# FFN first half: splitting the next block's input weights ahead of the block, and adding the second half of the converted weights behind that split

## The chip, the cores and the metric

The kernel runs on one core of one Trainium2 chip. The metric is the device time of one execution in microseconds. Before the change three executions took 719.34, 719.35 and 721.04 us (median 719.35 us).

## What is computed

A clustered attention feeds a two-layer FFN with a learned slope for negative values, and that feeds a routed mixture of experts. The change lies in the FFN:

```python
def _moe_ref(x, w_in, w_out, alpha):          # x 1536 x 512, w_in 512 x 2048, w_out 2048 x 512
    h = x @ w_in
    g = np.maximum(h, 0.0) + alpha * np.minimum(h, 0.0)
    return (g @ w_out).astype(np.float32)
```

The weights arrive as 64-bit words (float64 values). [...]

## The kernel before

**Tiles.** The 2048 hidden columns are 16 blocks `f` of 128. The 1536 tokens are two halves `gi` of 768, and a half is two chunks `c` of 384. The first half (`gi` 0) goes over all 16 blocks, then the second half does. The change is in the loop over the blocks 2 to 15 of the first half.

**One block on TensorE (PE).** `hidden(0, f, ...)` makes `h` for chunk 0 and chunk 1: each is 12 matmuls (line 677), four with the high input weights `wh` and the high tokens, four with `wh` and the low tokens, four with the low weights `wl`. The two PSUM tiles `h` come from a pool of two buffers, so chunk c of block f+1 needs the tile that chunk c of block f left. Then `second(0, f - 1)` adds 18 matmuls (line 726) of the block before to six sums `y`.

**One chunk on the other engines.** VectorE (DVE) makes `gm` from `h` (lines 702 and 703; the last reader of `h` is line 703), ScalarE (ACT) rounds it to `gh` (line 705), DVE subtracts: `gl = gm - gh` (line 707).

**Conversion.** `convert(f + 2)` stands behind chunk 1 of block f. It works in two halves of 128x512: q = 0 are the block's input weights, q = 1 its output weights. ACT takes the absolute value (line 569) and the top bits (line 570), DVE clamps (571), shifts (573) and joins (575), and GpSimd (POOL) adds the two pieces (line 577). `word` is a generator with these steps, and `convert` steps both halves in turn:

```python
            for _ in range(4):
                for g in gs:
                    next(g, None)
```

**Split.** `split(f, o, eng)` makes `wh` on ACT (line 648) and `wl = w - wh` on `eng` (line 649); o = 0 are the input weights, o = 1 the output weights. In the loop `eng` is GpSimd. Behind chunk 0 of block f stand `split(f + 1, 0)` and `split(f, 1)`.

**What sets the order.** Each engine works through its own queue in the order in which the code issues instructions; `hidden` calls `after(c)` behind each chunk. SP's queue brings a block's 64-bit weights with `load(f + 5)`, behind `hidden`.

Of the kernel before, what the change touches and what calls it, by code (L numbers as in the profile page):

```python
# [543 lines left out]
class Convert:  # L544
# [10 lines left out]
    def load(self, f):  # L555
        raw = self.slot(f)
        self.nc.sync.dma_start(out=raw[:, :DM].rearrange("p (k n) w -> p k (n w)", k=DM // P), in_=self.w_in[:, :, f])
        self.nc.sync.dma_start(out=raw[:, DM:].rearrange("p n w -> p (n w)"), in_=self.w_out[:, f])
# [53 lines left out]
def ffn(tc, A, cst, xs, xp, y1d, R, cv, W32, fw, ps_h, spare, more):  # L612
# [5 lines left out]
    nc = tc.nc  # L618
    ident, wg, LG = cst["ident"], cst["wg"], R["LG"]
    KD = DM // P  # L620
    NF = DFF // P
# [8 lines left out]
    def convert(f):  # L630

        if f < NF:
            gs = [cv.word(f, slice(q * DM, (q + 1) * DM), ck.tile([P, DM], I32, tag="ct", name="ct")) for q in range(2)]
            for _ in range(4):
                for g in gs:
                    next(g, None)

    ws, gs, over = {}, {}, {}

    def split(f, o, eng, gi=0):  # L640

        if o == 1 and gi == 1 and NF - TAIL <= f < NF - 2:
            wh, wl = over["xl"].pop(0), over["xl"].pop(0)
        else:
            wh = fw.tile([P, DM], F32R, tag=f"wh{o}", name=f"wh{o}")
            wl = fw.tile([P, DM], F32R, tag=f"wl{o}", name=f"wl{o}")
        w = W32(f)[:, o * DM:(o + 1) * DM]
        nc.scalar.copy(wh, w)
        eng.tensor_tensor(out=wl, in0=w, in1=wh.bitcast(F32), op=ALU.subtract)  # L649
        ws[f, o] = (wh, wl)  # L650
# [7 lines left out]
    def hidden(gi, f, eng, after, between=lambda: None):  # L658
        for _ in hiddens(gi, f, eng, after, between):
            pass  # L660

    def hiddens(gi, f, eng, after=lambda c: None, between=lambda: None, act=False):
# [17 lines left out]
        for c in range(2):  # L680
# [29 lines left out]
            if not act or f + c == 2:  # L710
                pay()
            after(c)
            if c == 1:
                gs[f] = (gh, gl)
# [4 lines left out]
    def second(gi, f, ns=range(3), ts=range(GT)):  # L719
        wh, wl = ws[f, 1]  # L720
        gh, gl = gs[f]
        for n, (a, w) in enumerate(((gh, wh), (gh, wl), (gl, wh))):
            for t in ts if n in ns else ():
                if f == 0 and n == 0:
                    ys[gi * GT + t] = ps_y.tile([P, DM], F32, tag="y", name="y")
                nc.tensor.matmul(ys[gi * GT + t], lhsT=a[:, t * P:(t + 1) * P], rhs=w,  # L726
                                 start=(f == 0 and n == 0), stop=(gi == 0 and f == NF - 1 and n == 2))
        if ns[-1] == 2 and ts[-1] == GT - 1:
            del ws[f, 1], gs[f]
# [60 lines left out]
    for f in (4, 5, 6):  # L790
        load(f)
    convert(3)
    second(0, 0)
    for f in range(2, NF):

        def after(c):
            if c == 0:
                split((f + 1) % NF, 0, nc.gpsimd)
                split(f, 1, nc.gpsimd)
            else:  # L800
                convert(f + 2)

        hidden(0, f, nc.vector, after)
        if f + 5 < NF:
            load(f + 5)
        second(0, f - 1)
# [742 lines left out]
def kernel(ctx, tc, A):  # L1549
# [164 lines left out]
    def begin():  # L1714
        ps_h = c2.enter_context(tc.tile_pool(name="ps_h", bufs=2, space=PSUM, side="right", reuse_waits="tile"))
        fw = c0.enter_context(tc.tile_pool(name="ffw", bufs=2, side="right", reuse_waits="tile"))
        return ffn(tc, A, cst, xs, xp, y1d, R, cv, lambda f: w32[f], fw, ps_h, spare, lambda *a: got.append(a) if a else more())
# [108 lines left out]
```

## Time and profile before

| | |
|---|---|
| median of three executions | 719.35 us |
| profiled execution, its own time | 718.92 us |
| its span in the trace | 717.1 us |
| attention with the FFN's first two blocks beside its end | to 263.5 us |
| blocks 2 to 15 of the first half of the tokens | 263.5 to 382.0 us |
| second half of the tokens | 382 to 504 us |
| routing and experts | from 504 us |

The profiled execution's time is 1.8 us more than its span (what lies around the span), and 0.43 us under the median. The page's first part gives each engine's busy time. A timeline row gives start, duration, engine, line, operation, and in brackets how long the engine was idle before it and who ended that.

### The profile page before, as it was taken

How to read it: one execution, taken by the hardware profiler on the slowest of the kernel's cores; microseconds unless marked ns; L12 is line 12 of the kernel's file. 1: busy time of each engine (PE TensorE's matmuls, PEld its weight loads, DVE VectorE, ACT ScalarE, POOL GpSimd, SP SyncE). 2: the span in 40 equal slices, each digit the busy share in tenths (PEclk: the TensorE clock that was granted, in tenths of full speed). 3: DMA queues.
4: the chain of work that ended last, by engine and by line, in shares of the span. 5: the costliest groups of instructions: out<-in, count | busy, mean ns of one | idle time of the engine just before them, and what ended most of it. 6: DMA issues, size and time to landing. Idle time of an engine off the chain costs nothing.

```text
span 717.1 us, 11778 instructions
## 1 busy us (share of the span) xinstructions
PE 699.9 (98%) x4111; PEld 625.8 (87%) x4111; DVE 568.2 (79%) x1114; ACT 472.1 (66%) x905; POOL 381.9 (53%) x339
## 2 busy tenths in 40 slices
PE   8999999999999999999999999999999999999995
PEld 5998989989999899888889999999888989898884
DVE  6989988898989878788784989976468888785651
ACT  6889788888889954554545655556645867574640
POOL 4659779697896386666662000001025888884201
PEclk9999999999999999999999999999999999999998
DMA  7867666676765133333203600026444999996000
GB/s 204 213 160 177 133 166 157 156 173 127 169 164 123 41 115 122 133 138 136 119 1 122 188 0 1 1 64 202 147 149 139 385 367 320 353 352 262 33 10 25
DMA packets 43904, 108.42 MB, mean 151 GB/s; under 512 B 8698, under 2 KB 24522, under 8 KB 38464
## 3 DMA queue, kind: packets, MB, share of 16 engines
q1 hardware_dynamic: 36768, 67.03, 34.4%
q0 software_dynamic: 7072, 40.60, 15.3%
q8 instruction: 34, 0.56, 0.3%
q14 instruction: 30, 0.25, 0.1%
HBM read 74.78 MB, written 10.10 MB: 118 GB/s over the span
## 4 chain that ended last, share of the span: by engine, by line
PE 66%; DVE 8%; DMA 8%; ACT 6%; POOL 6%; issue 5%; POOLq 0%; SPq 0%; ACTq 0%; DVEq 0%
PE h L677 18%; PE y L726 16%; DMA raw<-in_wall_dram,wi 7%; PE yo L1210 5%; PE pt L342 4%; PE hw L1263 4%; PE h L1210 3%; PE s L308 2%; PE px L360 2%; DVE nm L324 2%; PE y L736 2%; ACT e L331 2%; PE s L311 2%; DVE etl L345 2%; PE px L362 2%
## 5 line engine op out<-in xcount | busy, mean ns | idle before, releaser
L345 DVE TENSOR_TENSOR etl<-pt,eth 128x384 fp32r<-128x384 f32 x192 | 101.9, 549 | 19.6 <-ACT eth L344 18.4
L344 ACT CAST eth<-pt 128x384 fp32r<-128x384 f32 x192 | 90.9, 485 | 19.4 <-PE pt L342 19.4
L1177 POOL DMA_INDIRECT xg<-y1d,gi x16 | 27.8, 1738 | 130.5 <-DVE gi L1026 113.8
L342 PE MATMUL pt<-ident,e 128*128 128x128 f32 x576 | 93.8, 272 | 0.3 <-ACT e L331 0.3
L331 ACT ACTIVATE e<-s,nm 128x768 f32<-128x768 f32 x96 | 87.4, 910 | 6.4 <-DVE nm L324 5.6
L324 DVE TENSOR_REDUCE nm<-s 128x1 f32<-128x768 f32 x96 | 90.5, 943 | 0.9 <-PE s L311 0.8
L705 ACT CAST gh<-gm 128x384 fp32r<-128x384 f32 x60 | 30.8, 513 | 81.8 <-DVE gm L703 58.5
L342 PEld LDWEIGHTS pt<-ident,e 128*128 128x128 f32 x576 | 73.6, 140 | 7.0 <-ACT e L331 0.6
L707 DVE TENSOR_TENSOR gl<-gm,gh 128x384 fp32r<-128x384 f32 x60 | 49.4, 824 | 25.7 <-ACT gh L705 25.7
L360 PE MATMUL px<-etl,vh 128*64 128x384 f32 (+1 forms) x192 | 65.5, 368 | 1.5 <-DVE etl L345 1.3
L308 PE MATMUL s<-AB 128*128 128x384 f32 x192 | 57.5, 381 | 2.5 <-ACT e L331 2.1
L577 POOL TENSOR_TENSOR pre<-ct,pre 128x512 int32<-128x512 int32 x26 | 37.2, 1451 | 35.8 <-DVE ct L575 35.8
L677 PE MATMUL h<-xh,wh 128*128 128x384 f32 x256 | 55.6, 338 | 0.6 <-DVE gm L700 0.4
L677 PE MATMUL h<-xh,wl 128*128 128x384 f32 x256 | 56.0, 339 | 0.0
L677 PE MATMUL h<-xl,wh 128*128 128x384 f32 x256 | 55.0, 336 | 0.0
L362 PE MATMUL px<-eth,vh 128*128 128x384 f32 x160 | 54.0, 337 | 0.0
L1545 DVE TENSOR_TENSOR wl<-raw,wh 128x2048 fp32r<-128x2048 f32 (+2 forms) x26 | 44.5, 1717 | 11.7 <-ACT wh L1541 11.7
L311 PE MATMUL s<-CD 128*128 128x384 f32 x192 | 49.3, 338 | 1.0 <-DVE CD L439 1.0
L677 PEld LDWEIGHTS h<-xh,wh 128*128 128x128 f32 x256 | 45.5, 188 | 3.3 <-DVE gm L700 0.5
L677 PEld LDWEIGHTS h<-xh,wl 128*128 128x128 f32 x256 | 44.6, 188 | 2.7 <-POOL wl L649 2.6
L677 PEld LDWEIGHTS h<-xl,wh 128*128 128x128 f32 x256 | 45.7, 188 | 0.0
L1541 ACT CAST wh<-raw 128x2048 fp32r<-128x2048 f32 (+2 forms) x26 | 37.4, 1444 | 10.6 <-PE yo L1210 10.6
(357 smaller groups left out, 1816.8 us busy)
## 6 DMA issues: line engine op xcount, KB each, us to landing
AB<-RL SPq DMA_DIRECT2D x31, 384.0 KB, 5.3
raw<-in_w_in_dram SPq DMA_DIRECT2D x16, 512.0 KB, 4.0
raw<-in_w_out_dram SPq DMA_DIRECT2D x16, 512.0 KB, 4.7
raw<-in_wall_dram SPq DMA_DIRECT2D x8, 1024.0 KB, 8.2
Tp<-in_qkT_dram SPq DMA_DIRECT2D x16, 384.0 KB, 4.1
CD<-RL SPq DMA_DIRECT2D x15, 384.0 KB, 6.9
raw<-in_wall_dram POOLq DMA_DIRECT2D x4, 1024.0 KB, 11.8
vt<-in_v_dram SPq DMA_DIRECT2D x8, 384.0 KB, 6.3
```

The costliest lines, as they stand in the source:

```text
L308: nc.tensor.matmul(s[:, u, :384], lhsT=AB[:, 0, t * P:(t + 1) * P], rhs=AB[:, 1, ks], start=True, stop=False)
L311: nc.tensor.matmul(s[:, u, :384], lhsT=CD[:, 0, t * P:(t + 1) * P], rhs=CD[:, 1, ks], start=False, stop=True)
L324: nc.vector.tensor_reduce(out=nm, in_=s[:, :, :384], axis=AX.XY, op=ALU.max, negate=True)
L331: nc.scalar.activation(e.rearrange("p (u c) -> p u c", u=2), s[:, :, :384], AF.Exp, bias=nm, accum_out=den[:, i % 3:i % 3 + 1])
L342: nc.tensor.transpose(pt[:, i2], e[:, kt * P:(kt + 1) * P], ident)
L344: nc.scalar.copy(eh, pt)
L345: lows[u] = lambda: nc.vector.tensor_tensor(out=etl[:, 3 * u:3 * u + 3, q * P:(q + 1) * P], in0=pt, in1=eh.bitcast(F32), op=ALU.subtract)
L360: nc.tensor.matmul(px[:m], lhsT=vh[:, kt, :m], rhs=etl[:, kt], start=False, stop=False)
L362: nc.tensor.matmul(px, lhsT=vh[:, kt, :], rhs=eth[:, kt], start=False, stop=(kt == NT - 1))
L677: nc.tensor.matmul(hs[c], lhsT=a[:, k * P:(k + 1) * P], rhs=x[:, k, c * HC:(c + 1) * HC], start=(k == 0 and i == 0), stop=(k == KD - 1 and ...
L726: nc.tensor.matmul(ys[gi * GT + t], lhsT=a[:, t * P:(t + 1) * P], rhs=w, start=(f == 0 and n == 0), stop=(gi == 0 and f == NF - 1 and n == 2))
L1210: nc.tensor.matmul(out, lhsT=l[:, k], rhs=r[:, k * DM:(k + 1) * DM], start=start and k == 0 and i == 0, stop=stop and k == 3 and i == len( ...
```

## The change

`convert` leaves out the last step (the POOL add) of its second half and keeps its generator in `sums`. At the head of the loop's body, before `hidden`, now stand `split(f + 1, 0)` (until now behind chunk 0) and, behind it, that add. `split(f, 1)` stays behind chunk 0. No instruction is added or removed, and none changes its operands or size.

```diff
         if f < NF:
             gs = [cv.word(f, slice(q * DM, (q + 1) * DM), ck.tile([P, DM], I32, tag="ct", name="ct")) for q in range(2)]
-            for _ in range(4):
-                for g in gs:
+            for n in range(4):
+                for g in gs if n < 3 else gs[:1]:
                     next(g, None)
-
+            sums.append(gs[1])
+
+    sums = []
...
         def after(c):
             if c == 0:
-                split((f + 1) % NF, 0, nc.gpsimd)
                 split(f, 1, nc.gpsimd)
             else:
                 convert(f + 2)
 
+        split((f + 1) % NF, 0, nc.gpsimd)
+        for g in sums:
+            next(g, None)
+        sums.clear()
         hidden(0, f, nc.vector, after)
```

In the changed file lines 648, 649, 705 and 707 are 650, 651, 707 and 709.

On ACT, from the conversion of block 5 to the second chunk of block 4, before (`ct`, `pre`: the conversion; `gh`: chunk 0, then chunk 1 of block 4; the first `wh` is block 5's input weights, the second block 4's output weights; what stands in brackets is whose signals an instruction waits for):

```order
L569 ACTIVATE ct<-raw_3816 128x512 [waits DMAHW2_49,Pool_49]
L570 ACTIVATE pre_3818<-raw_3816 128x512
L705 CAST gh<-gm 128x384 [waits DVE_49,PE_49,Activation_49]
L648 CAST wh_4059<-pre_3818 128x512 [waits Pool_49]
L648 CAST wh_4063<-pre_3818 128x512 [waits PE_49]
L705 CAST gh<-gm 128x384 [waits DVE_49]
```

The same place on ACT in the changed kernel:

```order
L569 ACTIVATE ct<-raw_3816 128x512 [waits DMAHW2_49,Pool_49]
L570 ACTIVATE pre_3818<-raw_3816 128x512
L650 CAST wh_4038<-pre_3818 128x512 [waits PE_49,Pool_49]
L707 CAST gh<-gm 128x384 [waits DVE_49,PE_49,Activation_49]
L650 CAST wh_4063<-pre_3818 128x512 [waits PE_49]
L707 CAST gh<-gm 128x384 [waits DVE_49]
```

The `wh` of the next block's input weights, which waits for POOL, has moved from behind `gh` of chunk 0 to ahead of it.

On POOL, the conversions of blocks 5 and 6 and the splits around them, before:

```order
L577 TENSOR_TENSOR pre_3818<-ct,pre_3818 128x512 [waits DVE_49,Activation_49] x2
L649 TENSOR_TENSOR wl_4060<-pre_3818,wh_4059 128x512 [waits PE_49,Activation_49]
L649 TENSOR_TENSOR wl_4064<-pre_3818,wh_4063 128x512 [waits Activation_49]
L577 TENSOR_TENSOR pre_3819<-ct,pre_3819 128x512 [waits DVE_49,Activation_49] x2
L649 TENSOR_TENSOR wl_4140<-pre_3819,wh_4139 128x512 [waits PE_49,Activation_49]
L649 TENSOR_TENSOR wl_4144<-pre_3818,wh_4143 128x512 [waits Activation_49]
```

The same place on POOL in the changed kernel:

```order
L577 TENSOR_TENSOR pre_3818<-ct,pre_3818 128x512 [waits DVE_49,Activation_49]
L651 TENSOR_TENSOR wl_4039<-pre_3818,wh_4038 128x512 [waits PE_49,Activation_49]
L577 TENSOR_TENSOR pre_3818<-ct,pre_3818 128x512 [waits DVE_49]
L651 TENSOR_TENSOR wl_4064<-pre_3818,wh_4063 128x512 [waits Activation_49]
L577 TENSOR_TENSOR pre_3819<-ct,pre_3819 128x512 [waits DVE_49,Activation_49]
L651 TENSOR_TENSOR wl_4119<-pre_3819,wh_4118 128x512 [waits PE_49,Activation_49]
L577 TENSOR_TENSOR pre_3819<-ct,pre_3819 128x512 [waits DVE_49]
L651 TENSOR_TENSOR wl_4144<-pre_3818,wh_4143 128x512 [waits Activation_49]
```

The second add of each conversion has moved behind the low part of the input weights; PE's and DVE's own orders are as before.

## Rows read from the trace of the kernel before

**Rows 1.** The page, part 1: busy time, share of the span, instructions.

```profile
PE 699.9 (98%) x4111; PEld 625.8 (87%) x4111; DVE 568.2 (79%) x1114; ACT 472.1 (66%) x905; POOL 381.9 (53%) x339
```

**Rows 2.** Busy time by stretch: PE, PEld, DVE, ACT, POOL, granted clock, DMA share.

```profile
263.50:382.00 118.50, 118.50 (x589) 105.36 (x588) 97.07 (x163) 59.12 (x110) 79.86 (x58) 1.00 0.28 98
```

**Rows 3.** PE timeline, blocks 2 to 15: start, duration, line, operation.

```profile
263.50 0.87 PE L677 MATMUL h<-xh,wh 128*128 128x384 f32 x4
...
271.81 0.87 PE L677 MATMUL h<-xh,wh 128*128 128x384 f32 x4
...
347.92 0.86 PE L677 MATMUL h<-xh,wh 128*128 128x384 f32 x4
348.62 0.86 PE L677 MATMUL h<-xl,wh 128*128 128x384 f32 x4
349.41 0.97 PE L677 MATMUL h<-xh,wl 128*128 128x384 f32 x4
...
373.52 0.87 PE L677 MATMUL h<-xh,wh 128*128 128x384 f32 x4
...
375.82 0.85 PE L677 MATMUL h<-xh,wh 128*128 128x384 f32 x4
```

**Rows 4.** Who waited for whom, 246 to 382 us: total, times, longest.

```profile
PEld h L677 <- POOL wl L649: 2.6, 10, 0.3
```

**Rows 5.** POOL timeline: the first and the last conversion's adds (blocks 3 and 15).

```profile
268.23 2.86 POOL L577 TENSOR_TENSOR pre<-ct,pre 128x512 int32<-128x512 int32 x2 [1.70 <-DVE ct L575]
...
370.52 2.87 POOL L577 TENSOR_TENSOR pre<-ct,pre 128x512 int32<-128x512 int32 x2 [2.82 <-DVE ct L575]
```

**Rows 6.** POOL timeline from block 12's conversion on; the x2 row begins with the x1 row.

```profile
344.94 1.61 POOL L577 TENSOR_TENSOR pre<-ct,pre 128x512 int32<-128x512 int32 x1 [2.84 <-DVE ct L575]
346.51 1.28 POOL L577 TENSOR_TENSOR pre<-ct,pre 128x512 int32<-128x512 int32 x1
347.76 1.60 POOL L649 TENSOR_TENSOR wl<-pre,wh 128x512 fp32r<-128x512 f32 x1
347.76 2.85 POOL L649 TENSOR_TENSOR wl<-pre,wh 128x512 fp32r<-128x512 f32 x2
```

**Rows 7.** DVE timeline over the same block: end of block 12's conversion, block 11's chunks.

```profile
344.11 1.29 DVE L575 SCALAR_TENSOR_TENSOR ct<-raw,ct 128x512 int32<-128x512 int32 x2
344.71 0.69 DVE L575 SCALAR_TENSOR_TENSOR ct<-raw,ct 128x512 int32<-128x512 int32 x1
...
345.96 0.56 DVE L703 SCALAR_TENSOR_TENSOR gm<-h,gm 128x384 f32<-128x384 f32 x1
347.17 1.04 DVE L707 TENSOR_TENSOR gl<-gm,gh 128x384 fp32r<-128x384 f32 x1 [0.66 <-ACT gh L705]
...
348.77 0.56 DVE L703 SCALAR_TENSOR_TENSOR gm<-h,gm 128x384 f32<-128x384 f32 x1
349.91 1.12 DVE L707 TENSOR_TENSOR gl<-gm,gh 128x384 fp32r<-128x384 f32 x1 [0.58 <-ACT gh L705]
```

**Rows 8.** ACT timeline over the same block.

```profile
346.62 0.51 ACT L705 CAST gh<-gm 128x384 fp32r<-128x384 f32 x1 [2.99 <-DVE gm L703]
347.04 1.14 ACT L648 CAST wh<-pre 128x512 fp32r<-128x512 f32 x2
...
350.91 0.66 ACT L569 ACTIVATE ct<-raw 128x512 f32<-128x512 f32 x1
```

**Rows 9.** Timelines, block 15 and later: `gl` with POOL idle, and two hand-offs.

```profile
378.41 0.56 DVE L707 TENSOR_TENSOR gl<-gm,gh 128x384 fp32r<-128x384 f32 x1 [0.66 <-ACT gh L705]
...
378.28 0.62 ACT L648 CAST wh<-w32a 128x512 fp32r<-128x512 f32 x1
...
378.98 1.30 POOL L649 TENSOR_TENSOR wl<-w32a,wh 128x512 fp32r<-128x512 f32 x1 [2.77 <-ACT wh L648]
...
494.43 0.56 DVE L700 SCALAR_TENSOR_TENSOR gm<-h,Tp 128x384 f32<-128x384 f32 x1 [0.48 <-ACT Tp L699]
...
495.04 0.65 PEld L677 LDWEIGHTS h<-xh,wh 128*128 128x128 f32 x4 [0.50 <-DVE gm L700]
```

## Prediction

> **What bounds the kernel now.** I read the page's first part first: PE is busy 98% of the span [rows 1], so a change helps only where it takes time off PE's queue, and hurts only where it stops PE. Then the busy time by stretch: in the changed stage PE shows no idle time and a granted clock of 1.00 [rows 2]. A busy PE hides short waits of its weight loads, so next I read its timeline. Block 2 takes 271.81 - 263.50 = 8.31 us; from block 2 to block 15 it is (373.52 - 263.50) / 13 = 8.463 us. So about 0.155 us a block, 2.0 us in 13 blocks, is lost. It goes ahead of the matmuls with the low weights: in block 12 they start 0.79 us behind the group before them, where that group follows its own predecessor at 0.70 [rows 3]. The waits name the cause: the weight load waited for POOL's `wl` ten times, 2.6 us in all [rows 4].
>
> Why is `wl` late? Look at POOL: from the first add of block 3's conversion to that of block 15 it is 370.52 - 268.23 = 102.29 us in 12 turns, 8.52 us each [rows 5], against PE's 8.31 without waits. DVE, ACT and POOL are a ring of their own, slower than PE by 0.2 us a block, and PE touches it now and then through `wl`. That ring is what the change rearranges, so I follow one turn of it from T = 344.94, the start of block 12's first add. All times from here to the sum are from T, and the conversion's halves are q0 and q1:
>
> - POOL: add q0 0 to 1.61, add q1 1.57 to 2.85, `wl` of the next block 2.82 to 4.42, `wl` of the output weights to 5.67 [rows 6].
> - DVE: line 703 of chunk 0 ends at 1.58, `gl` runs 2.23 to 3.27; line 703 of chunk 1 ends at 4.39, its `gl` at 6.09 [rows 7]. These are chunks of block 11, whose `h` is long there: PE starts block 12 at 347.92 [rows 3]. DVE waits for ACT, not for PE.
> - ACT: `gh` of chunk 0 1.68 to 2.19, then two `wh` [rows 8].
> - From `gl` of chunk 0 (3.27) to the next add (8.52) it is 5.25 us: DVE lines 702 and 703 of chunk 1, ACT's `gh` and three conversion steps, DVE's lines 571, 573 and 575.
>
> The reader should lay the DVE rows beside the POOL rows. `gl` takes 0.56 us with POOL idle [rows 9], and 1.04 and 1.12 here. Chunk 0's ends at 348.21, 0.42 us after add q1 ended (347.79); chunk 1's at 351.03, 0.42 us after the second `wl` ended (347.76 + 2.85 = 350.61) [rows 6, 7]. So `gl` stands still until the POOL instruction then running has ended, and needs 0.42 us more. In return, the `wl` that starts while `gl` finishes takes 1.60 instead of 1.28 us.
>
> This is the lock of the Trainium skill, "SBUF — State Buffer", section "SBUF: two separate sides": a DVE instruction with two SBUF inputs and a GpSimd instruction that reads SBUF share one port pair, and whichever starts first holds it for the whole instruction. The trace agrees (0.42 us, twice per block). If the two shared bandwidth instead, the sum below would be the 6.1 us of the first rival.
>
> **The change, part by part.** Nothing is added; three things move.
>
> *`wh` ahead of `gh` on ACT.* `wh` of the next block's input weights needs POOL's add q0, which ends at 1.61. Before, ACT did `gh` of chunk 0 at 1.68 and `wh` behind it. Now `gh` stands behind `wh`, and waits though its own input is there at 1.58. The trace of before has no ACT wait on POOL in this stage. The hand-offs that it has are 0.05 us (POOL to PE, 349.36 to 349.41, [rows 3, 6]), 0.08 us (ACT to POOL, 378.90 to 378.98, [rows 9]), 0.10 us (DVE to ACT, 346.52 to 346.62, [rows 7, 8]) and 0.14 us (DVE to POOL, 344.11 + 0.69 = 344.80 to 344.94, [rows 6, 7]). I take 0.06, nearest the one that POOL gives, with 0.05 and 0.14 as ends. So `wh` runs 1.67 to 2.29, and `gh` starts 0.52 us behind its start (two `wh` take 1.14, one 0.62): 2.19 to 2.70. That is 0.51 us later than before.
>
> *`wl` ahead of add q1 on POOL.* `wl` starts 0.08 us after `wh`: at 2.37. No DVE instruction with two SBUF inputs runs then, so it takes 1.28: to 3.65. (Its bounds are 1.28 and 1.60; 1.60 belongs to a start under a `gl`, and that is now add q1.) `gl` is ready at 2.74, in the middle of it, and stands still to 3.65: it ends at 3.65 + 0.42 = **4.07, where it was 3.27: 0.80 us later**.
>
> *add q1 behind it.* It starts at 3.62 under `gl`'s end, so 1.60: to 5.22. The second `wl` runs 5.19 to 6.47, chunk 1's `gl` ends at 6.89, that is 2.82 us behind chunk 0's `gl`, as before (6.09 - 3.27). So the remaining 5.25 us of the ring keep their shape, and the next add q0 starts at 4.07 + 5.25 = **9.32 instead of 8.52**.
>
> *What is behind the waits.* On ACT, `wh` of the output weights and `gh` of chunk 1 come later by 0.5 and 0.8 us; the second comes from DVE anyway. The buffer of add q1 is free at 5.22, and ACT refills it at 5.97 (350.91, [rows 8]) + 0.80 = 6.77. PE needs the output weights' `wl` (6.47) only in `second`, behind all of the next `hidden`. SP's loads move with the blocks; they are five blocks ahead. `split(0, 0)` for the second half moves up in block 15, where nothing waits for it. All this I cost at nothing; of the covers the buffer's is the thinnest, 1.5 us, and past it each us would add a us to the ring.
>
> *Where PE stops.* The wait for `wl` goes: it is ready at 3.65, not at 4.42. What is late next is the PSUM tile: chunk 1 of the next block needs line 703 of chunk 1. That ends at 4.39 before, and PE comes at 375.82 - 370.52 = 5.30 [rows 3, 5]: 0.9 us of slack. Now it ends at 4.39 + 0.80 = 5.19, in a ring that falls 1.0 us a block behind PE (9.32 - 8.31). So by block 4 PE stands there, and then goes at the ring's pace.
>
> *The sum.* 12 turns of the ring [rows 5]: 12 x 0.80 = 9.6 us. At the end PE's chunk 1 of block 15 came at 5.30 from T; now at 5.19 + 0.05 (DVE to PE, 494.99 to 495.04, [rows 9]) + about 0.1 for the restart (a group behind a wait takes 0.97 instead of 0.86, [rows 3]) = 5.34. So +9.6 us stays; the second half moves along whole behind PE. On the profiled execution: 718.92 + 9.6 = 728.5; on the median of the three runs, 0.43 higher: **729.0 us**. With the ends of the hand-off it is 12 x 0.79 to 12 x 0.88: 9.5 to 10.6 us.
>
> **Rivals.**
>
> 1. *Only ACT's order counts*: `gl` isn't held by `wl`. Then the ring grows by the 0.51 us of `gh`: 12 x 0.51 = 6.1 us, 725.4 us. Against it stand the two ends at +0.42 us; for it, that one of them is behind an add and one behind the other `wl`, and neither behind this one.
> 2. *`wl` is slowed too*: 1.60 instead of 1.28 us. The ring grows by 1.12, 13.4 us, 732.8 us. It would need a DVE access in the first 0.3 us of `wl`, where DVE now waits for ACT.
> 3. *Not slower*: the wait for `wl` goes and the ring doesn't grow. This needs `gh` of chunk 0 not to be held: add q0 would have to end at 1.02 or before, 0.6 us ahead of line 703, so that `wh` is out of the way by 1.6; it ends at 1.61. If it were so, PE would run on to the PSUM tile's slack: -0.9 us, 718.5 us; and if `gl` then also slipped in at 2.23, before `wl`, and needed 0.56 (an end at 2.79 for 3.27), the ring would be 8.04 us, below PE's 8.31, and all 2.0 us would come back: 717.3 us. For it speaks that the 2.6 us of PE waits are real and go. Against it: ACT keeps its order even with a finished input (the second `wh` of [rows 8], whose input was added a block earlier, stands behind 2.99 us of idle time).
>
> **How the numbers follow.** What a measurement of this kernel can tell from no change is about 0.3%, 2.2 us. Forecast 0.74, rival 1 0.11, rival 2 0.07, rival 3 0.08. The forecast and rivals 1 and 2 are slower by over 0.3%: 0.92. Rival 3 gives at most 2.0 us, within 0.3%: 0.06 of its 0.08; I leave 0.02 for more. The range takes in the forecast with the ends of its hand-off (728.9 to 730.0) and rival 1, with 0.4 and 1.0 us beyond, and leaves out rivals 2 and 3 (0.15): 725.0 to 731.0.
>
> **What would show it.** In the profile after: POOL's first adds 9.3 us apart from block 3 to block 15; ACT waiting for POOL's add ahead of `wh`, 13 times; DVE's wait for `gh` of chunk 0 near 1.2 us instead of 0.66, that `gl` near 1.3 us long and ending 0.42 us behind `wl`; no PE wait for `wl`, but about 1 us a block for DVE's line 703 (705 in the new file), from block 4 on; the stage from 263.5 near 128 us long; DVE, ACT and POOL busy about as before. Wrong would be a ring of 9.0 (rival 1), of 9.6 (rival 2), or of 8.5 us and less (rival 3).

## The result, and the profile after

The changed kernel takes 728.69 us (median of six runs, 726.99 to 730.03), the kernel before 719.35 us (717.52 to 721.04, six runs). The ratio is 1.0132, with a 95% interval of 1.0111 to 1.0154: slower by 9.3 us, where 9.6 were forecast. The profiled execution took 726.99 us, with a span of 725.2 us.

The page's first part for the changed kernel, which answers to [rows 1]:

```profile
PE 702.1 (97%) x4111; PEld 624.5 (86%) x4111; DVE 570.6 (79%) x1114; ACT 472.5 (65%) x905; POOL 381.9 (53%) x339
```

The same work on every engine, to within 2.5 us. The time is in waits, so this view can't tell where. The busy time by stretch can, if the stretch runs from the same matmul to the same matmul: from the first of block 2 to the first behind the loop over the blocks 2 to 15. First the kernel before, then the changed one (columns as in [rows 2]; PEld are PE's weight loads):

```profile
263.50:382.02 118.52, 118.52 (x589) 105.36 (x588) 97.07 (x163) 59.12 (x110) 79.89 (x58) 1.00 0.28 98
```

```profile
262.21:390.06 127.85, 121.66 (x589) 104.53 (x588) 99.99 (x163) 59.17 (x110) 80.13 (x58) 1.00 0.26 91
```

The stage takes 127.85 instead of 118.52 us, +9.33 us, and PE, which showed no idle time, now shows 6.2 us. The granted clock stays at 1.00. (The profiled execution came to the stage 1.3 us sooner than the one of before, so its span is only 8.1 us longer.) Behind the stage, from the first matmul of the second half to the end of the span, nothing grew: 717.1 - 384.75 = 332.4 us before, 725.2 - 392.78 = 332.4 us after.

Who waited for whom in the changed kernel, 246 to 391 us (answers to [rows 4]):

```profile
ACT wh L650 <- POOL pre L577: 39.4, 13, 3.9
...
DVE gl L709 <- ACT gh L707: 26.1, 32, 1.1
...
PEld h L679 <- DVE gm L705: 10.0, 12, 0.9
...
PEld h L679 <- ACT wh L650: 3.6, 11, 0.3
```

The weight loads' wait for POOL's `wl` is gone, as the change intends. In its place they wait 12 times for DVE's last reading of the PSUM tile, 10.0 us in all, and 11 times for `wh`. At the head of it stands ACT, which waits 13 times for POOL's first add.

One turn of the ring in the changed kernel: POOL, then DVE, then ACT, then PE (start, duration, line; answers to [rows 6, 7, 8, 3]):

```profile
350.63 1.61 POOL L577 TENSOR_TENSOR pre<-ct,pre 128x512 int32<-128x512 int32 x1 [2.85 <-DVE ct L575]
352.98 1.29 POOL L651 TENSOR_TENSOR wl<-pre,wh 128x512 fp32r<-128x512 f32 x1 [0.73 <-ACT wh L650]
354.22 1.60 POOL L577 TENSOR_TENSOR pre<-ct,pre 128x512 int32<-128x512 int32 x1
355.78 1.29 POOL L651 TENSOR_TENSOR wl<-pre,wh 128x512 fp32r<-128x512 f32 x1
359.92 1.61 POOL L577 TENSOR_TENSOR pre<-ct,pre 128x512 int32<-128x512 int32 x1 [2.85 <-DVE ct L575]
```

```profile
351.65 0.56 DVE L705 SCALAR_TENSOR_TENSOR gm<-h,gm 128x384 f32<-128x384 f32 x1
353.35 1.33 DVE L709 TENSOR_TENSOR gl<-gm,gh 128x384 fp32r<-128x384 f32 x1 [1.14 <-ACT gh L707]
...
355.24 0.56 DVE L705 SCALAR_TENSOR_TENSOR gm<-h,gm 128x384 f32<-128x384 f32 x1
356.38 1.11 DVE L709 TENSOR_TENSOR gl<-gm,gh 128x384 fp32r<-128x384 f32 x1 [0.58 <-ACT gh L707]
```

```profile
352.28 0.62 ACT L650 CAST wh<-pre 128x512 fp32r<-128x512 f32 x1 [2.95 <-POOL pre L577]
352.80 0.51 ACT L707 CAST gh<-gm 128x384 fp32r<-128x384 f32 x1
```

```profile
352.95 0.98 PE L679 MATMUL h<-xh,wh 128*128 128x384 f32 x4
...
355.86 0.96 PE L679 MATMUL h<-xh,wh 128*128 128x384 f32 x4 [0.52 <-DVE gm L705]
```

From T = 350.63 the reader finds the forecast's steps: add q0 ends at 1.61; `wh` 1.65 (forecast 1.67); `gh` 2.17 (2.19); `wl` 2.35 to 3.64 (2.37 to 3.65); `gl` of chunk 0 ends at 354.68, 4.05 (4.07), that is 0.41 us behind the end of `wl`; line 705 of chunk 1 ends at 5.17 (5.19), and PE's chunk 1 starts at 5.23 (5.24). The first and the last conversion's first add (answer to [rows 5]):

```profile
266.93 1.61 POOL L577 TENSOR_TENSOR pre<-ct,pre 128x512 int32<-128x512 int32 x1 [1.70 <-DVE ct L575]
...
378.53 1.61 POOL L577 TENSOR_TENSOR pre<-ct,pre 128x512 int32<-128x512 int32 x1 [2.85 <-DVE ct L575]
```

(378.53 - 266.93) / 12 = 9.30 us a turn, where 9.32 was forecast and 8.52 was before.

### The profile page after: what moved, and what is told of

Read it like the earlier page. It is cut to its first block, busy times and chain, and to the rows that moved or that the text cites. A ratio compares the mean times of both kernels' runs of the same rounds, so it can differ in the third digit from the quotient of the medians.

```text
span 725.2 us, 11778 instructions
## 1 busy us (share of the span) xinstructions
PE 702.1 (97%) x4111; PEld 624.5 (86%) x4111; DVE 570.6 (79%) x1114; ACT 472.5 (65%) x905; POOL 381.9 (53%) x339
## 4 chain that ended last, share of the span: by engine, by line
PE 48%; DVE 16%; ACT 10%; POOL 9%; issue 8%; DMA 8%; POOLq 0%; ACTq 0%; DVEq 0%
PE h L679 9%; PE y L728 7%; DMA raw<-in_wall_dram,wi 7%; PE yo L1215 5%; PE pt L342 4%; PE hw L1268 4%; POOL pre L577 3%; PE h L1215 3%; DVE gl L709 3%; PE s L308 2%; PE px L360 2%; PE y L738 2%; ACT ct L569 2%; DVE nm L324 2%; PE s L311 2%
## 5 line engine op out<-in xcount | busy, mean ns | idle before, releaser
L709 DVE TENSOR_TENSOR gl<-gm,gh 128x384 fp32r<-128x384 f32 x60 | 52.3, 872 | 31.9 <-ACT gh L707 31.9
L679 PE MATMUL h<-xh,wh 128*128 128x384 f32 x256 | 58.1, 348 | 6.8 <-DVE gm L705 6.2
L577 POOL TENSOR_TENSOR pre<-ct,pre 128x512 int32<-128x512 int32 x26 | 41.8, 1606 | 36.0 <-DVE ct L575 36.0
L650 ACT CAST wh<-pre 128x512 fp32r<-128x512 f32 x50 | 30.8, 618 | 44.7 <-POOL pre L577 39.4
L679 PEld LDWEIGHTS h<-xh,wh 128*128 128x128 f32 x256 | 43.9, 188 | 16.1 <-DVE gm L705 10.0
```

Source lines behind the costliest of these rows:

```text
L577: nc.gpsimd.tensor_tensor(out=w, in0=t, in1=w, op=ALU.add)
L679: nc.tensor.matmul(hs[c], lhsT=a[:, k * P:(k + 1) * P], rhs=x[:, k, c * HC:(c + 1) * HC], start=(k == 0 and i == 0), stop=(k == KD - 1 and ...
L709: eng.tensor_tensor(out=gl[:, o], in0=m, in1=gh[:, o].bitcast(F32), op=ALU.subtract)
```

## The experiments

A timeline can agree with a wrong reason. The first two kernels take the two moves apart; the next two take away what is said to make `gl` stand still and leave every order as it is; the last two look for the gain that the stage still holds. A time is the median of that kernel's runs. Its ratio is to runs of the kernel before made beside them (medians 718.63 us for the first four, 719.59 us for the last two); it is estimated from all runs, with a 95% interval, and so is not just the quotient of two medians.

**The early split alone.** Both adds stay together; only the split moves ahead of the block.

```diff
         def after(c):
             if c == 0:
-                split((f + 1) % NF, 0, nc.gpsimd)
                 split(f, 1, nc.gpsimd)
...
+        split((f + 1) % NF, 0, nc.gpsimd)
         hidden(0, f, nc.vector, after)
```

> The early split alone: the split of the next block's input weights stands ahead of the block, but both adds of a conversion stay together, as before the change. So ACT's order is that of the change and POOL's order that of before. Theory (the loss needs both moves, since a low-part instruction that reads SBUF must be running when the first chunk's gl comes): gh of chunk 0 comes 0.51 us later and DVE waits about 1.15 us for it instead of 0.66, but gl then stands still until the second add ends, as before; the ring stays at 8.5 us a block and the time at about 719.4 us (718.5 to 720.5). Rival (ACT's order is what costs, 0.51 us a turn): a ring of 9.0 us and about 725.4 us. Rival (early wh by itself stops PE): 728.

Measured: 719.75 us, ratio to before 0.9999 (0.9980 to 1.0017). The ring took (372.39 - 270.04) / 12 = 8.53 us. ACT, DVE and POOL in one turn:

```profile
348.45 0.62 ACT L648 CAST wh<-pre 128x512 fp32r<-128x512 f32 x1 [2.95 <-POOL pre L577]
348.97 0.51 ACT L705 CAST gh<-gm 128x384 fp32r<-128x384 f32 x1
```

```profile
349.51 0.58 DVE L707 TENSOR_TENSOR gl<-gm,gh 128x384 fp32r<-128x384 f32 x1 [1.12 <-ACT gh L705]
```

```profile
346.81 2.85 POOL L577 TENSOR_TENSOR pre<-ct,pre 128x512 int32<-128x512 int32 x2 [2.84 <-DVE ct L575]
```

`gh` is as late as in the change, and DVE waits 1.12 us for it. But POOL runs the second add meanwhile, to 349.66, and behind that `gl` could not have ended before 349.66 + 0.42 = 350.08 in any case: it ends at 350.09. The late `gh` uses up time in which `gl` stood still before. So ACT's order by itself doesn't cost 0.51 us a turn. Whether this `wl` would hold `gl`, which the first rival denies, this kernel can't tell, since POOL runs the second add at that place.

**The late add alone.** The second add stands behind the low part of the input weights, but that split stays behind chunk 0 (against the changed kernel):

```diff
             if c == 0:
+                split((f + 1) % NF, 0, nc.gpsimd)
+                for g in sums:
+                    next(g, None)
+                sums.clear()
                 split(f, 1, nc.gpsimd)
...
-        split((f + 1) % NF, 0, nc.gpsimd)
-        for g in sums:
-            next(g, None)
-        sums.clear()
         hidden(0, f, nc.vector, after)
```

> The late add alone: the second add stands behind the low part of the next block's input weights, but that split stays behind chunk 0. ACT's order is that of before and POOL's order that of the change. Theory: gl of chunk 0 now falls into POOL's gap (the first add ends at 1.61 from T, the low part cannot start before 2.8), runs undisturbed 2.23 to 2.79 instead of ending at 3.27; but everything on POOL is then later, chunk 1's gl stands still behind the second add (to about 5.8) and the conversion's first DVE step (line 571), which comes at about 5.7, behind the second low part (to about 7.0). The ring is 8.8 to 9.1 us and the time 722.5 to 725.5 us: slower than before, but less than the change. Rival (only the early wh costs): the wait for the low part goes, 717.3 to 718.5 us. Rival (the late add by itself is the cost): 728.7 us.

Measured: 723.27 us, ratio 1.0058 (1.0036 to 1.0081). The first adds of the conversions lie (374.52 - 267.00) / 12 = 8.96 us apart. DVE and POOL in the turn from T = 338.66; the last row of DVE is chunk 0's `gl` of the turn behind it:

```profile
343.16 1.27 DVE L709 TENSOR_TENSOR gl<-gm,gh 128x384 fp32r<-128x384 f32 x1 [0.58 <-ACT gh L707]
344.35 1.86 DVE L571 TENSOR_SCALAR ct<-ct 128x512 f32<-128x512 f32 x2
...
349.86 0.56 DVE L709 TENSOR_TENSOR gl<-gm,gh 128x384 fp32r<-128x384 f32 x1 [0.66 <-ACT gh L707]
```

```profile
342.71 1.30 POOL L577 TENSOR_TENSOR pre<-ct,pre 128x512 int32<-128x512 int32 x1
343.98 1.61 POOL L651 TENSOR_TENSOR wl<-pre,wh 128x512 fp32r<-128x512 f32 x1
```

Chunk 0's `gl` (349.86) takes its bare 0.56 us in POOL's gap: that part is a gain. It is lost again behind: chunk 1's `gl` stands still behind the second add, and line 571 behind the second `wl`, to 345.59, which is 6.93 from T (7.0 was expected). The two moves are no sum: alone they cost 0 and 0.6%, together 1.3%. What PE then meets the expectation did not name: its weight loads wait for ACT's `wh` (12 times, 9.1 us), not for the PSUM tile.

**The change with `gl` fed from PSUM.** DVE's second step writes over `h`; all orders are the change's:

```diff
-                nc.vector.scalar_tensor_tensor(out=m, in0=h, scalar=0.0, in1=m, op0=ALU.max, op1=ALU.add)
+                nc.vector.scalar_tensor_tensor(out=h, in0=h, scalar=0.0, in1=m, op0=ALU.max, op1=ALU.add)
+                m = h
```

> The change, with the second step of the chunk's nonlinearity (line 705) writing its result over h in PSUM instead of into an SBUF tile, so that gl has one SBUF input instead of two; the orders of all engines are those of the change. Theory (gl is held because it has two SBUF inputs while POOL works): gl of chunk 0 takes about 0.56 us and ends at about 3.3 from T instead of 4.07; the ring is about 8.55 us. PE gets the PSUM tile only when gl has ended, so it comes about 0.4 us later once: about 720.2 us (719.3 to 721.5). Rival (the loss is gh behind wh on ACT, or POOL's order, and gl's length is only a symptom): between 725 and 729 us, with a ring of 9.0 to 9.3 us.

Measured: 719.16 us, ratio to before 1.0003 (0.9986 to 1.0019), a turn of (369.02 - 267.65) / 12 = 8.45 us. DVE and POOL:

```profile
346.36 0.56 DVE L710 TENSOR_TENSOR gl<-h,gh 128x384 fp32r<-128x384 f32 x1 [1.09 <-ACT gh L708]
```

```profile
346.02 1.29 POOL L651 TENSOR_TENSOR wl<-pre,wh 128x512 fp32r<-128x512 f32 x1 [0.73 <-ACT wh L650]
347.27 1.30 POOL L577 TENSOR_TENSOR pre<-ct,pre 128x512 int32<-128x512 int32 x1
```

`gl` comes 0.34 us after `wl` began, as in the change (0.37), and now runs beside it in 0.56 us. The second add is no longer slowed either: 1.30 instead of 1.60 us. One SBUF input less on `gl`, and the loss is gone although ACT and POOL keep the change's order. That shows that `gl`, standing still beside POOL, made the loss. (ACT's `gh` reads PSUM now too, and takes 0.47 instead of 0.51 us: too little for it. Time and ring are a little under what was expected, 719.3 to 721.5 and 8.55 us; the ratio can't be told from 1.)

**The kernel before with `gl` fed from PSUM** (the same edit).

> The kernel before, with the same edit (line 703 writes over h in PSUM, gl has one SBUF input). Theory: gl of chunk 0 no longer stands still behind the second add and ends at 2.8 instead of 3.27 from T; the ring alone would take about 8.05 us, less than PE's 8.31, so PE sets the pace, its wait for the low part goes and the 2.0 us of that stage come back: about 717.3 us (716.8 to 718.3). Rival (the ring's length has nothing to do with gl's standing still): 719.4 us, with the ring still at 8.5 us.

Measured: 716.38 us, ratio 0.9962 (0.9946 to 0.9979): faster than both kernels, and 0.4 us under the range that was expected. The ring took 7.97 us a turn up to block 12 ((339.73 - 267.96) / 9) and then kept PE's pace ((364.52 - 347.91) / 2 = 8.31). The stage:

```profile
263.24:379.53 116.29, 116.29 (x589) 105.89 (x588) 86.08 (x163) 58.04 (x110) 76.63 (x58) 1.00 0.29 100
```

116.29 instead of 118.52 us, with PE busy throughout: 8.31 us for each of the 14 blocks. DVE is busy 11 us less, for the most part because a `gl` that stands still counts as busy.

**The late add, with the output weights' low part on DVE** (against the late add alone). `high` makes `wh` as `split` does; its subtraction runs on DVE between line 705 and `gl` of chunk 1.

```diff
-                split(f, 1, nc.gpsimd)
+                high(f)
...
+        lows.append(lambda: nc.vector.tensor_tensor(out=wl, in0=w, in1=wh.bitcast(F32), op=ALU.subtract))
...
-        hidden(0, f, nc.vector, after)
+        hidden(0, f, nc.vector, after, low)
```

> The late add alone, and the low part of the output weights made by DVE (between line 705 of chunk 1 and chunk 1's gl) instead of by POOL: POOL has three instructions a block left instead of four. Theory: gl of chunk 0 still runs in POOL's gap, and nothing of POOL's stands in the way of line 571 any more; the ring alone takes about 8.0 us, PE sets the pace at 8.31, and the time is 2 us below that of the kernel before (ratio 0.996 to 0.999), about 5 us below the late add alone. Rival (DVE is simply full, so that 0.7 us more on it lengthens its turn): a ring of 9 us or more and 723 us or more.

Measured: 717.28 us, ratio 0.9969 (0.9950 to 0.9987). The time is as expected, the ring is not: (367.38 - 266.71) / 12 = 8.39 us instead of 8.0. DVE and POOL show why:

```profile
312.48 0.81 DVE L661 TENSOR_TENSOR wl<-pre,wh 128x512 fp32r<-128x512 f32 x1
313.22 1.65 DVE L723 TENSOR_TENSOR gl<-gm,gh 128x384 fp32r<-128x384 f32 x1
```

```profile
311.45 1.29 POOL L651 TENSOR_TENSOR wl<-pre,wh 128x512 fp32r<-128x512 f32 x1 [1.19 <-ACT wh L650]
312.69 1.76 POOL L577 TENSOR_TENSOR pre<-ct,pre 128x512 int32<-128x512 int32 x1
```

The second add starts under DVE's `wl` and is slowed to 1.76 us, and chunk 1's `gl` stands still behind that add. A ring only 0.08 us slower than PE's 8.31 met PE in the last blocks alone (8.32 us a block on average).

**The kernel before with the second add in two halves.**

```diff
-        nc.gpsimd.tensor_tensor(out=w, in0=t, in1=w, op=ALU.add)
+        for s in (slice(0, DM // 2), slice(DM // 2, DM)) if o.start else (slice(0, DM),):
+            nc.gpsimd.tensor_tensor(out=w[:, s], in0=t[:, s], in1=w[:, s], op=ALU.add)
```

> The kernel before, with the second add of each conversion issued as two POOL instructions of 256 columns instead of one of 512. If gl stands still for the POOL instruction that is running, and no longer, it gets in after the first half: gl of chunk 0 ends at about 2.8 from T instead of 3.27. The extra instruction costs POOL about 0.25 us, and line 571 meets the end of the second low part; the ring alone comes to about 8.3 us, so the time is 1 to 2 us below before (ratio 0.997 to 0.999). Rival (the two share bandwidth, or gl waits for POOL's queue to run empty): no gain, ratio 1.000 or more, gl of chunk 0 as long as before or longer.

Measured: 716.8 us, ratio 0.9962 (0.9944 to 0.9980). That is a little more gain than was expected (0.997 to 0.999), but the interval reaches into that range. The turn is (366.66 - 267.64) / 12 = 8.25 us, where 8.3 was expected. DVE and POOL from T = 308.88; the first row of POOL holds all three adds, the two below it are the halves of the second:

```profile
311.12 0.56 DVE L708 TENSOR_TENSOR gl<-gm,gh 128x384 fp32r<-128x384 f32 x1 [0.66 <-ACT gh L706]
...
313.38 0.56 DVE L708 TENSOR_TENSOR gl<-gm,gh 128x384 fp32r<-128x384 f32 x1 [0.58 <-ACT gh L706]
314.02 1.69 DVE L571 TENSOR_SCALAR ct<-ct 128x512 f32<-128x512 f32 x2
```

```profile
308.88 3.39 POOL L578 TENSOR_TENSOR pre<-ct,pre 128x512 int32<-128x512 int32 x3 [2.03 <-DVE ct L575]
...
310.45 0.74 POOL L578 TENSOR_TENSOR pre<-ct,pre 128x256 int32<-128x256 int32 x1
...
311.15 1.13 POOL L578 TENSOR_TENSOR pre<-ct,pre 128x256 int32<-128x256 int32 x1
```

POOL has more to do (3.39 us for the adds instead of 2.85) and nothing less, and yet the kernel is faster: `gl` of chunk 0 is ready as the first half ends (311.12 and 311.19), gets in ahead of the second, and ends at 311.68, 2.80 from T, where 2.8 was expected; the second half is the slowed one (1.13 us, the first 0.74). So `gl` waits for the POOL instruction that is running, not for POOL to run empty.

## Why the prediction was right

- **The bound.** "DVE, ACT and POOL are a ring of their own, slower than PE": right. In the kernel before the stage's 2 us come back when the ring alone gets shorter than 8.31 us (8.25 with the add in halves, 7.97 with `gl` fed from PSUM): with both the stage takes the same 116.29 us, so a still shorter ring gains nothing. The time rises with the ring where it is longer (8.96 and 9.30 us).
- **`wh` ahead of `gh`.** The hand-off from POOL to ACT, taken as 0.06 us between 0.05 and 0.14, is 352.28 - 352.24 = 0.04. That and the rest of the turn make 9.30 for 9.32. By itself the move costs nothing, as the early split alone showed; the prediction gave it 0.51 us of `gh` and let it count only through `gl`, which was right.
- **`wl` ahead of the second add.** The step on which the sum hung was that `gl` would stand still for this `wl` too, though in the trace of before it stood behind other instructions. It did (0.41 us behind its end), and with `gl` fed from PSUM the loss was gone. Nor do the two share: whether 0.62, 0.92 or 1.23 us of POOL's instruction were left when `gl` became ready (before; after; the late add with `wl` on DVE), `gl` ended 0.41 to 0.42 us behind it. The first rival (725.4 us) falls with that. The second (1.60 us for `wl`) falls with 1.29 us. One thing in the prediction is not exact: a `gl` that stood quite still until POOL's end would need its whole 0.56 us from there. Why it needs 0.14 less, no run shows.
- **Where PE stops.** At the PSUM tile of chunk 1, from block 4 on (281.45 there, after a wait of 0.68 us), as said. Not foreseen was the second stop in each block, 0.3 us for `wh` at chunk 0. PE now comes to a block as soon as the ring lets it, and `wh` is ready only at 2.3 from T. It costs nothing more, since chunk 1 stops later anyway; it only takes its part of that stop (10.0 us in 12 times, 0.83 each, where about 1 us was said).
- **The size.** Forecast +9.6 us, stage +9.33, median +9.3. The 0.3 us between are 0.02 us in each of the 12 turns (111.60 - 102.29 = 9.31 us for 12 x 0.80), and the hand-off from POOL to ACT, 0.04 instead of 0.06, is about as much.
- **The third rival** (not slower) needed add q0 to end 0.6 us before line 703; it ends 0.03 us behind it (1.61 and 1.58), now as before.

The change does what it was made for: `wl` is ready 0.8 us sooner from T and PE never waits for it. But `wl` was late because the ring was slow, and the change made the ring slower.

## What to carry to other kernels

Where several engines feed a full PE, the wait that PE shows can be the place where a slower ring touches it; before moving the late piece earlier, measure the ring's turn (one instruction, first to last, divided by the turns) and ask whether the move shortens it. An instruction that stands still while another engine's runs is not just late or early: what counts is whose instruction is running when it becomes ready, so compare ends, and look for an instruction whose end keeps a fixed distance to another engine's end. Here one input taken from PSUM, or one POOL instruction cut in two, was worth more than any order of the same instructions that was tried.

## What the runs showed of the hardware

- A DVE subtraction with two SBUF inputs (128x384) takes 0.56 us alone, and ends 0.41 to 0.42 us behind the POOL instruction that was running when it became ready (0.49 where that one ended only 0.07 us after `gl` became ready, as in the halves). With one input in PSUM it takes 0.56 us beside POOL, and POOL's instruction 1.30 instead of 1.60 us. The first was read from the trace of before, the second was not known.
- A DVE instruction with a single SBUF input is held too: two of line 571 (0.43 us each alone) took 1.86 us behind a POOL subtraction in the late add, and 1.69 with the add in halves. The first of the two in the late add ended at 345.87, 0.28 us behind POOL (345.59). So one SBUF input instead of two freed `gl`, but the number of inputs alone doesn't say which DVE instruction is held.
- How far behind POOL a held DVE instruction ends goes with its own length: 0.28 us for line 571 (0.43 alone), 0.42 for `gl` (0.56 alone), 0.55 for DVE's own `wl` of the last but one experiment (313.29 and 312.74; 0.69 alone, in the second half of the tokens). Each is 0.14 to 0.15 us less than the time alone.
- POOL's first add of a conversion takes 1.61 us in every run, where the second takes 1.30 with nothing beside it. The first begins 0.46 us before DVE's second line 575 ends, which has two SBUF inputs (350.63 and 351.09 in the changed kernel). That this is the reason, and 0.3 us of the ring, no run tested.
- PE idled for some 0.5 us in each of 12 blocks, and the granted clock stayed at 1.00.
